# Seven products of halves for a part of the first DFT, the second DFT as a stage of its own, and block sums made by transfers

## The chip, the cores and the metric

The kernel runs on one core of one Trainium2 chip, all in 32-bit floating point. The metric is device time in microseconds (us) of one execution. The kernel before takes 946.69 us, the median of three runs (946.5 to 949.13).

## What is computed

One block of a network on x of 2048 rows s by 512 columns d (the batch is 1):

```
def _A_ref(x, dft_seq_re, dft_seq_im, dft_hid_re, dft_hid_im):
    a = jnp.einsum("bsd,ed->bse", x, dft_hid_re)
    b = jnp.einsum("bsd,ed->bse", x, dft_hid_im)
    return jnp.einsum("ts,bse->bte", dft_seq_re, a) - jnp.einsum("ts,bse->bte", dft_seq_im, b)

def _B_ref(x, w_in, w_sp, b_sp, w_out):
    z = _gelu(jnp.einsum("bsd,df->bsf", x, w_in))             # f: 2 * 896
    z1, z2 = z[..., :896], _layernorm(z[..., 896:], axis=-1)
    g = jnp.einsum("ts,bsf->btf", w_sp, z2) + b_sp[None, :, None]   # w_sp: 2048 x 2048
    return jnp.einsum("bsf,fd->bsd", z1 * g, w_out)

mod = (_silu(c) @ w_mod).reshape(c.shape[0], 6, 1, -1)
sa, ca, ga, sb, cb, gb = (mod[:, j] for j in range(6))
h = _layernorm(x, axis=-1) * (1 + ca) + sa
x = x + ga * _A_ref(h, A_dft_seq_re, A_dft_seq_im, A_dft_hid_re, A_dft_hid_im)
h = _layernorm(x, axis=-1) * (1 + cb) + sb
x = x + gb * _B_ref(h, B_w_in, B_w_sp, B_b_sp, B_w_out)
```

The kernel turns the order of the two transforms round: it first forms G = (C h), with C the real and the imaginary matrix over the rows s, and then multiplies G by the small matrices over the columns d.

## The kernel before

**Products.** A float32 factor is split into a high part (a copy in the TensorE's format, made by ScalarE) and a low part (the rest, made by VectorE), and each product of tiles is three matmuls, high by high, high by low and low by high (`matmul3`, lines 95 to 97). A matmul has 128 x 128 weights and 512 columns.

**Stages.** (1) The first DFT, tiles `gp`. The 2048 output positions are four row blocks t of 512. For each t and each of the real and imaginary matrices (j) there are 16 steps over s, 128 steps n in all, and a step is 4 column blocks of 128 by 3 matmuls, 12 matmuls. Its matrix arrives in blocks of 512 x 512 (tile `stage`, 1 MB, four transfers), which VectorE turns 32 x 32 by 32 x 32 (tile `t`) before ScalarE makes the high half (`ah`, line 256) and VectorE the low one (`al`, line 263). (2) The second DFT, tiles `yp`, 384 matmuls on G, which stays on the chip as `gh` and `gl`; its pieces are called between the steps of stage 1, a row block later. (3) z1 and z2, the two halves of the product with w_in. (4) The product with w_sp, tiles `gw`, as seven products of halves: it needs sums of quarters of w_sp, which VectorE makes from tiles `sj` and stores to `s_d` (`load_s`, `sum_s`, lines 756 to 769). (5) The product with w_out, tiles `op`.

**After a piece of the second DFT** (`post_y`, `norm_y`, `post_h`) VectorE adds the residual (`xr`) and takes mean and variance (`bn_stats`, lines 103 to 105), GpSimd makes the reciprocal root from them in three tiny instructions (`mvy`, `rsy`, `nmry`: lines 107, 108, 115), ScalarE normalizes (line 119), two elementwise passes multiply and add the modulation rows (lines 579, 580), and the result goes to DRAM.

**Order.** The engines run their instructions in the order in which the program writes them. A table (`at(n, function, arguments)`) says after which step n a piece of side work is written; `run(n)` writes it, and `prep(n)` writes the preparation of the factors some steps ahead. Tiles rotate through a fixed number of buffers (`bufs=`), and an instruction that writes a tile waits until the readers of the buffer's last tile are done. The SP queue issues the loads of the stages, the GpSimd (POOL) queue the stores and a few loads.

## Time and profile before

| | |
|---|---|
| median of three runs | 946.69 us |
| the profiled execution, first to last instruction | 945.0 us |
| TensorE busy | 938.0 us, 99% |
| VectorE busy | 707.0 us, 75% |
| ScalarE busy | 386.9 us, 41% |
| GpSimd busy | 177.4 us, 19% |
| moved by transfers | 161.79 MB, 171 GB/s over the span |
| first real matmul starts at | 8.01 us |
| last matmul starts at | 941.27 us |

The span is the time between the first and the last instruction of one execution that the profiler recorded; its 945.0 us lie 1.7 us below the median of the unprofiled runs. "Busy" is a sum over instructions whose ends can overlap the next one's start, so what one instruction costs in a row of instructions is read from start to start. The DMA share of a stretch is the mean busy share of the core's 16 transfer engines, and can come out a little over 1. In the table of groups, "idle before" is the time in which an engine stood still ahead of the group's instructions, with what ended the wait behind the arrow.

### The profile page before, as it was taken

The numbers are of one execution on the slowest core, as the hardware profiler recorded it, in microseconds if no ns is written. First come the engines' busy times: TensorE is split into PE (matmuls) and PEld (weight loads), VectorE is DVE, ScalarE is ACT, GpSimd is POOL, SyncE is SP. The second block draws the span as 40 slices with busy tenths as digits, with TensorE's granted clock in tenths as the row PEclk, the third lists the DMA queues.
The fourth block names the chain that finished last, engine by engine and source line by source line (L and its number), as shares of the span: only waits on it lengthen the run. The fifth ranks groups of instructions, "written<-read, shape, count | busy, mean of one in ns | idle before, by whom it ended". The sixth has DMA issues, their size and how long they took to land.

```text
span 945.0 us, 12296 instructions
## 1 busy us (share of the span) xinstructions
PE 938.0 (99%) x4158; PEld 780.9 (83%) x4158; DVE 707.0 (75%) x1048; ACT 386.9 (41%) x670; POOL 177.4 (19%) x333
## 2 busy tenths in 40 slices
PE   8999999999999999999999999999999999999998
PEld 6878888888888888888888999888888888888886
DVE  7789957775765657767978587877688688885872
ACT  3685424232232222322876356544544444331221
POOL 1430000221631145122323265200000000000000
PEclk9999999999999999999999999999999999999999
DMA  8998653577668965996398985555554456833541
GB/s 194 222 214 165 130 134 90 146 197 158 134 101 197 281 208 150 279 281 141 95 344 282 326 267 160 149 114 134 124 134 90 106 117 141 205 107 117 198 155 59
DMA packets 253230, 161.79 MB, mean 171 GB/s; under 512 B 134576, under 2 KB 222896, under 8 KB 253040
## 3 DMA queue, kind: packets, MB, share of 16 engines
q1 hardware_dynamic: 238544, 120.62, 53.7%
q0 software_dynamic: 12272, 39.61, 12.3%
q10 hardware_dynamic: 2352, 0.79, 0.3%
q8 instruction: 32, 0.52, 0.3%
q14 instruction: 30, 0.25, 0.1%
HBM read 124.26 MB, written 36.71 MB: 170 GB/s over the span
## 4 chain that ended last, share of the span: by engine, by line
PE 94%; DMA 2%; SPq 1%; issue 1%; POOL 1%; DVE 0%; ACT 0%; ACTq 0%; DVEq 0%; POOLq 0%
PE gp L96 11%; PE gp L97 11%; PE gp L95 11%; PE gw L95 10%; PE gw L96 10%; PE gw L97 10%; PE yp L97 3%; PE yp L96 3%; PE yp L95 3%; PE z2p L96 3%; PE z2p L95 3%; PE z2p L97 3%; PE op L97 3%; PE op L95 3%; PE op L96 3%; PE z1p L96 1%
## 5 line engine op out<-in xcount | busy, mean ns | idle before, releaser
L256 ACT ACTIVATE ah<-t 128x512 fp32r<-128x512 f32 x263 | 164.4, 627 | 310.2 <-PE gp L97 181.0
L263 DVE TENSOR_TENSOR al<-t,ah 128x512 fp32r<-128x512 f32 x264 | 179.9, 685 | 133.4 <-PE gp L96 59.8
L96 PE MATMUL gp<-al,hh 128*128 128x512 f32 x480 | 186.8, 389 | 1.2 <-DVE al L263 1.2
L97 PE MATMUL gp<-ah,hl 128*128 128x512 f32 x480 | 186.8, 389 | 0.0
L95 PE MATMUL gp<-ah,hh 128*128 128x512 f32 x480 | 186.7, 389 | 0.0
L97 PE MATMUL gw<-ah,bl 128*128 128x512 f32 x400 | 155.6, 389 | 0.0
L96 PE MATMUL gw<-al,bh 128*128 128x512 f32 x400 | 155.6, 389 | 0.0
L95 PE MATMUL gw<-ah,bh 128*128 128x512 f32 x400 | 155.6, 389 | 0.0
L96 PEld LDWEIGHTS gp<-al,hh 128*128 128x128 f32 x480 | 90.1, 188 | 20.4 <-DVE al L263 1.6
L95 PEld LDWEIGHTS gp<-ah,hh 128*128 128x128 f32 x480 | 90.1, 188 | 18.7
L97 PEld LDWEIGHTS gp<-ah,hl 128*128 128x128 f32 x480 | 90.1, 188 | 18.8 <-DVE hl L448 0.2
L97 PEld LDWEIGHTS gw<-ah,bl 128*128 128x128 f32 x400 | 75.1, 188 | 15.7
L95 PEld LDWEIGHTS gw<-ah,bh 128*128 128x128 f32 x400 | 75.1, 188 | 15.5
L96 PEld LDWEIGHTS gw<-al,bh 128*128 128x128 f32 x400 | 75.1, 188 | 15.5
L227 DVE STREAM_TRANSPOSE t<-stage 128x1024 f32<-128x1024 f32 x62 | 76.7, 1238 | 8.7 <-DMA stage<-in_A_dft_seq_re_dram 8.6
L221 DVE STREAM_TRANSPOSE t<-stage 128x1024 f32<-128x1024 f32 x56 | 69.3, 1238 | 0.1
L791 ACT ACTIVATE bh<-z 128x512 fp32r<-128x512 f32 (+1 forms) x56 | 32.8, 586 | 65.7 <-PE gw L96 65.7
L769 POOL DMA_DIRECT2D s_d<-sj x64 | 35.1, 550 | 107.5 <-DVE sj L761 80.7
L95 PE MATMUL yp<-hth,gh 128*128 128x512 f32 x128 | 49.8, 389 | 0.0
L96 PE MATMUL yp<-htl,gh 128*128 128x512 f32 x128 | 49.8, 389 | 0.0
L97 PE MATMUL yp<-hth,gl 128*128 128x512 f32 x128 | 49.8, 389 | 0.0
L96 PE MATMUL z2p<-wil,ah 128*128 128x448 f32 x128 | 46.7, 365 | 0.0
(210 smaller groups left out, 1448.0 us busy)
## 6 DMA issues: line engine op xcount, KB each, us to landing
sj<-in_B_w_sp_dram SPq DMA_DIRECT2D x32, 512.0 KB, 8.3
s_d<-sj POOLq DMA_DIRECT2D x64, 256.0 KB, 4.1
stage<-s_d SPq DMA_DIRECT2D x128, 128.0 KB, 2.9
stage<-in_A_dft_seq_re_dram SPq DMA_DIRECT2D x60, 256.0 KB, 5.4
stage<-in_A_dft_seq_im_dram SPq DMA_DIRECT2D x60, 256.0 KB, 5.9
stage<-in_B_w_sp_dram SPq DMA_DIRECT2D x96, 128.0 KB, 3.1
stage<-h_d SPq DMA_DIRECT2D x32, 256.0 KB, 6.4
xr<-in_A_x_dram POOLq DMA_DIRECT2D x16, 256.0 KB, 4.3
```

The source lines that it names most:

```text
L95: nc.tensor.matmul(acc, ah, bh, start=first, stop=False, skip_group_check=go_on)
L96: nc.tensor.matmul(acc, ah, bl, start=False, stop=False, skip_group_check=go_on)
L97: nc.tensor.matmul(acc, al, bh, start=False, stop=last, skip_group_check=go_on)
L221: nc.vector.transpose(t.rearrange("p r (b i) -> p r b i", i=32), st[:, :, :, 16 * k:16 * k + 32])
L227: nc.vector.transpose(t.rearrange("p k (b i) -> p k b i", i=32), st[:, :, 32 * k:32 * k + 64].rearrange("p b (k i) -> p k b i", k=2))
L256: nc.scalar.activation(AH[n], source(n), AF.Copy)
L263: nc.vector.tensor_tensor(AL[n], source(n), AH[n].bitcast(F32), op=ALU.subtract)
L769: nc.gpsimd.dma_start(s_d[m, r, g][b * P:(b + 1) * P, :], a)
L791: nc.scalar.activation(BH[p, k][:, :w], b_of(p, k), AF.Copy)
```

## The change

The first DFT's row block t = 0 stays as it was. For t = 1, 2, 3 the rows s of the lower half (8 of the 16 tiles), the four column blocks (as 2 x 2) and the two matrices' rows are taken as quarters, and a 2 x 2 by 2 x 2 product of quarters is made from seven products of sums of them (`mm_s`, 14 units of 12 matmuls) where eight were needed; the upper half is multiplied directly onto the same accumulators (`mm_k`, 8 units of 24 matmuls). A row block is then 168 + 192 = 360 matmuls and was 384. VectorE makes the sums of the matrix blocks (`sum_f`, 128 x 1024) and of h (`sum_v`). Factors are split as pairs of two steps, 128 x 1024 at once (`hi_unit`, `lo_unit`).

G no longer stays on the chip: it goes to DRAM (`out_g`, `out_k`, tiles `go` with two buffers, stores on the POOL queue) and is read back in 16 pieces (`load_g`). The second DFT is a loop of 16 pieces m after the first (`mm_y`, 24 matmuls each); the residual is copied into its accumulator ahead (`seed_y`), and the gate `mods[2]` is multiplied into the small matrix (`gate_ht`), so that the statistics are taken from the accumulator directly.

The sums of quarters of w_sp are no longer made by VectorE: rows are loaded, negated by ScalarE, stored, and summed in DRAM by 32 accumulating transfers of 512 KB, beside 24 plain stores and 8 copies from DRAM to DRAM of that size, all on the POOL queue and written at steps 29 to 98. Two of the seven products take the opposite sign in their splits (`hi_b`, `lo_b`).

The core of the diff:

```
-        if s == NS - 1:
-            for k in range(ND):
-                ps = GP.pop((t, j, k))
-                gt_hi[t, j, k] = GP_[0].tile([P, Q], F32R, tag=f"gh{j}_{k}", name=f"gh{t}_{j}_{k}")
-                gt_lo[t, j, k] = GP_[0].tile([P, Q], F32R, tag=f"gl{j}_{k}", name=f"gl{t}_{j}_{k}")
-                split(gt_hi[t, j, k], gt_lo[t, j, k], ps)
...
+    def pair_of(d, u, name):
+        if u not in d:
+            d[u] = pairs.tile([P, 2, Q], F32R, tag=name, bufs=3, name=f"{name}{u}")
+        return d[u]
...
+    def sum_f(t, p, m):
...
+        dst, a, b, op = {5: (f5, b12, b22, ALU.add), 7: (b12, b11, b12, ALU.subtract),
+                         6: (b11, f5, b11, ALU.subtract), 3: (b21, b21, b11, ALU.subtract)}[p]
+        nc.vector.tensor_tensor(dst, a, b, op=op)
...
+    def out_g(t, c, ps):
+        g = temp(f"go{t}_{c}")
+        nc.scalar.activation(g, ps, AF.Copy)
+        nc.gpsimd.dma_start(g_d[t][c], g)
...
+    def mm_s(t, i):
+        p, m = ORD[i // 2], i % 2
+        acc = {1: "c11", 2: "c11", 5: "v", 3: "v", 6: "u", 7: "u", 4: "u"}[p]
...
+        for c_ in range(2):
+            for f in range(2):
+                matmul3(C[acc, f], *form_v(p, 2 * m + c_, f), ph[:, c_, :], pl[:, c_, :],
+                        p in (1, 5) and m == 0 and c_ == 0, m == 1 and c_ == 1, p not in (1, 5))
...
+    def mm_k(t, i, m):
...
+        for k in range(ND):
+            acc = (("c11", "v"), ("u", "c22"))[j][k // 2]
+            matmul3(C[acc, k % 2], h_hi[s][:, k, :], h_lo[s][:, k, :], ph, pl, False, s == 7, True)
+
+    def out_k(t, j):
+        for f in range(2):
+            out_g(t, 4 * j + f, C["u" if j else "c11", f])
+        for f in range(2):
+            um = UM[t][:, 2 * j + f, :]
+            nc.vector.tensor_tensor(um, C["c22" if j else "v", f], um, op=ALU.add)
+            nc.gpsimd.dma_start(g_d[t][4 * j + 2 + f], um)
...
+    def load_g(m):
+        t, i = divmod(m, 4)
+        GR[m] = yp[0].tile([P, 8, P], F32, tag="gr", bufs=2, name=f"gr{m}")
+        nc.sync.dma_start(GR[m], g_d[t].rearrange("c p s -> p c s")[:, :, i * P:(i + 1) * P])
...
+    def split_g(m):
+        GH[m] = yp[0].tile([P, 8, P], F32R, tag="gh", bufs=3, name=f"gh{m}")
+        GL[m] = yp[0].tile([P, 8, P], F32R, tag="gl", bufs=2, name=f"gl{m}")
+        split(GH[m], GL[m], GR.pop(m))
...
+    def negate_s(b):
+        n = SJ.pop(b)
+        for j in range(2):
+            nc.scalar.activation(n[:, j], n[:, j], AF.Copy, scale=-1.0)
+        nc.gpsimd.dma_start(s_rows(1, b), n[:, 0])
+        nc.gpsimd.dma_start(s_rows(3, b), n[:, 0])
+        nc.gpsimd.dma_start(s_rows(2, b), n[:, 1])
+
+    def add_s(dst, src_):
+        nc.gpsimd.dma_start(dst, src_, accum_op=ALU.add)
...
+    for role, l, n, m in ((21, 5, 9, 11), (11, 7, 13, 15), (12, 12, 17, 19), (22, 16, 21, 23)):
+        atd(l, load_first, role)
+        atd(n, turn_s, 1, role, 0)
+        atd(m, turn_s, 1, role, 1)
...
+    for b, n in enumerate((29, 32, 35, 58, 61, 64, 67, 70)):
+        atd(n, load_s, b)
+        atd(n + 3, negate_s, b)
+        atd(n + 1, copy_s4, b)
+        atd(n + 8, sum_s1, b)
+        atd(n + 9, sum_s3, b)
+        atd(n + 18, sum_s2, b)
+        atd(n + 28, sum_s4, b)
...
+    for m in range(16):
+        n = Y0 + 2 * m
+        atd(n - 3, split_g, m)
+        atd(n - 2, seed_y, m)
+        if m + 2 < 16:
+            atd(n - 2.5, load_g, m + 2)
+            atd(n - 1.5, load_xr, m + 2)
+        atd(n + 2, post_y, m)
+        atd(n + 3, norm_y, m)
+        atd(n + 4, post_h, m)
```

**The order on VectorE around a piece of the second DFT.** Before, from line 568 (the product's gate) over the statistics to the low halves and turns of the first DFT that are woven in:

```order
L566 TENSOR_TENSOR y_0_1786<-yp_0_1_1757,y_0_0_1425 128x512
L568 TENSOR_TENSOR y_0_1786<-y_0_1786,mod_1732 128x512
L569 TENSOR_TENSOR xr_0_1666<-y_0_1786,xr_0_1666 128x512
L103 BN_STATS bsty<-xr_0_1666 128x6
L105 BN_AGGR mvy<-bsty 128x2
L263 TENSOR_TENSOR al_1800<-t_1736,ah_1772 128x512
L227 STREAM_TRANSPOSE t_1802<-stage_1645 128x1024
```

In the changed kernel, in the loop over m (`gl` is the low half of a piece of G, `h_2` and `h_3` the pieces normalized by ScalarE, `wl` and `wraw` the preparation of w_in):

```order
L105 BN_STATS bsty<-yp_3184 128x6
L107 BN_AGGR mvy<-bsty 128x2
L918 TENSOR_TENSOR wl_3258<-wraw_0_3125,wh_3257 128x1024
L93 TENSOR_TENSOR gl_3309<-gr_3206,gh_3308 128x1024
L826 TENSOR_TENSOR h_3_3306<-h_3_3306,mod_2755 128x512
L827 TENSOR_TENSOR h_3_3306<-h_3_3306,mod_2757 128x512
L105 BN_STATS bsty<-yp_3235 128x6
L107 BN_AGGR mvy<-bsty 128x2
L918 TENSOR_TENSOR wl_3313<-wraw_2_3130,wh_3312 128x1024
L93 TENSOR_TENSOR gl_3364<-gr_3260,gh_3363 128x1024
L904 TENSOR_TENSOR wraw_0_3125<-wraw_0_3125 128x2x384
L826 TENSOR_TENSOR h_4_3361<-h_4_3361,mod_2755 128x512
```

And on ScalarE in that loop, where `x_3` is the copy of the accumulator that goes to DRAM and line 806 the copy of the residual:

```order
L817 ACTIVATE x_3_3277<-yp_3184 128x512
L806 ACTIVATE yp_3289<-xr_3186 128x512
L121 ACTIVATE h_3_3306<-x_3_3277,nmry,rsy 128x512
L92 ACTIVATE gh_3308<-gr_3206 128x1024
L915 ACTIVATE wh_3312<-wraw_2_3130 128x1024
L817 ACTIVATE x_4_3332<-yp_3235 128x512
```

What stood behind the statistics was work of the first DFT; what stands there now is `gl`, the low half of the piece of G that TensorE takes two pieces later, and it reads `gh`, which ScalarE writes behind the normalization of the same statistics.

**The order on VectorE at the start.** Before, around the statistics of x's third quarter (`bstx<-x_399`):

```order
L263 TENSOR_TENSOR al_529<-t_486,ah_511 128x512
L227 STREAM_TRANSPOSE t_531<-stage_338 128x1024
L103 BN_STATS bstx<-x_399 128x6
L105 BN_AGGR mvx<-bstx 128x2
...
L263 TENSOR_TENSOR al_570<-t_486,ah_538 128x512
L263 TENSOR_TENSOR al_593<-t_531,ah_572 128x512
L227 STREAM_TRANSPOSE t_595<-stage_448 128x1024
```

In the changed kernel (`pl` is the low half of a pair, `f_21` a quarter for the seven products of t = 1, whose block `sb_426` is loaded at step 5):

```order
L543 STREAM_TRANSPOSE tp_509<-stage_312 128x1024
L471 TENSOR_TENSOR hl_528<-xn_416,hh_498 128x512
L543 STREAM_TRANSPOSE f_21_531<-sb_426 128x1024
L105 BN_STATS bstx<-x_399 128x6
L107 BN_AGGR mvx<-bstx 128x2
...
L619 TENSOR_TENSOR pl_565<-tp_509,ph_563 128x1024
L543 STREAM_TRANSPOSE tp_567<-stage_340 128x1024
```

A turn of a block of the next row block now stands ahead of the statistics and of the pair that steps 14 and 15 multiply.

**The order of the POOL queue at steps 40 to 60.** Before, it held the first loads of the residual and, some steps on, the stores of x:

```order
L504 DMA w_1_1419<-hrow_d_132 128x512
L544 DMA xr_0_1666<-in_A_x_dram 128x512
L544 DMA xr_1_1711<-in_A_x_dram 128x512
L570 DMA x_d_76<-xr_0_1666 128x512
L107 TENSOR_SCALAR mvy<-mvy 128x1
```

Now, with `s_d` the sums of w_sp, `go` the copies of G and `um` the kept products that G's other half is made from:

```order
L1015 DMA s_d_0_95<-s_d_0_97 128x1024
L1015 DMA s_d_0_99<-in_B_w_sp_dram 128x1024
L1015 DMA s_d_0_97<-s_d_0_99 128x1024 x2
L654 DMA g_d_77<-go_0_1550 128x512
L654 DMA g_d_77<-go_1_1553 128x512
L708 DMA g_d_77<-um_1154 128x512 x2
L1015 DMA s_d_0_97<-s_d_0_99 128x1024
L1015 DMA s_d_0_101<-s_d_0_97 128x1024
```

The stores of G of the row block t = 1 stand behind the transfers that sum w_sp.

718 lines of the change are left out of this document (451 added, 267 removed).

## The prediction, made before the changed kernel was run

> **What bounds the kernel now.** I read the page first (the span, the engines' sums, the DMA queues, the chain that ended last, the costliest groups):
>
> ```profile
> span 945.0 us, 12296 instructions
> ...
> PE 938.0 (99%) x4158; PEld 780.9 (83%) x4158; DVE 707.0 (75%) x1048; ACT 386.9 (41%) x670; POOL 177.4 (19%) x333
> ...
> q1 hardware_dynamic: 238544, 120.62, 53.7%
> q0 software_dynamic: 12272, 39.61, 12.3%
> ...
> PE 94%; DMA 2%; SPq 1%; issue 1%; POOL 1%; DVE 0%; ACT 0%; ACTq 0%; DVEq 0%; POOLq 0%
> ...
> L96 PE MATMUL gp<-al,hh 128*128 128x512 f32 x480 | 186.8, 389 | 1.2 <-DVE al L263 1.2
> ```
>
> TensorE is the bound: 99% busy, 94% of the chain, and its largest group waited 1.2 us in all. Then the table by stretch (PE busy and its count, PEld, DVE, ACT, POOL, granted clock, DMA share, GB/s):
>
> ```profile
> 40.00:50.00 10.00, 9.40 (x42) 7.46 (x40) 3.58 (x8) 4.69 (x11) 4.14 (x14) 1.00 1.19 226
> 50.00:60.00 10.00, 9.38 (x41) 7.79 (x42) 9.82 (x15) 9.50 (x22) 2.74 (x9) 1.00 1.21 210
> ...
> 150.00:200.00 50.00, 50.00 (x222) 41.39 (x221) 38.84 (x58) 16.83 (x28) 6.98 (x14) 1.00 0.55 138
> ```
>
> A full TensorE does 222 matmuls in 50 us, 0.225 us each at clock 1.00 (the 389 ns are overlapping ends). The two stretches at 40 to 60 us show the one place where it waits, 0.6 us each; transfers are saturated there (share 1.2). So a removed matmul is worth 0.225 us, and only where the other engines keep up with the shorter work.
>
> **The gain.** Stage 1 loses 24 matmuls in each of three row blocks, 72 of 4158: 72 x 0.225 = 16.2 us. Nothing else leaves TensorE. In stages 3 to 5 what changes is the signs of two splits and 45 us of VectorE's sums, off the path while TensorE is full: nothing. Against the profiled execution that is 945.0 - 16.2 = 928.8 us if TensorE stays full.
>
> **The second DFT as a loop.** This is where I think it doesn't. Before, the statistics of a piece had a whole row block of other work behind them. Now a piece m costs TensorE 24 x 0.225 = 5.40 us, and the engines beside it form a ring: statistics of piece m on VectorE, three GpSimd instructions, normalization on ScalarE, and behind that in ScalarE's order the high half of G's piece m + 3; VectorE's next instruction is the low half of this piece, then the two modulation passes of piece m, and only then the statistics of m + 1. The links, from one piece before, engine by engine (start, length):
>
> ```profile
> 176.67 0.69 DVE L103 BATCH_NORM_STATS2 bsty<-xr 128x6 f32<-128x512 f32 x1
> 177.40 0.18 DVE L105 BATCH_NORM_AGGREGATE mvy<-bsty 128x2 f32<-128x6 f32 x1
> ```
>
> ```profile
> 177.68 0.54 POOL L107 TENSOR_SCALAR mvy<-mvy 128x1 f32<-128x1 f32 x1 [0.20 <-DVE mvy L105]
> 178.31 0.56 POOL L108 TENSOR_TENSOR rsy<-mvy,mhalf 128x1 f32<-128x1 f32 x1
> 178.97 0.27 POOL L115 TENSOR_SCALAR nmry<-mvy,rsy 128x1 f32<-128x1 f32 x1
> ```
>
> ```profile
> 179.27 0.82 ACT L119 ACTIVATE h<-xr,nmry,rsy 128x512 f32<-128x512 f32 x1 [1.37 <-POOL nmry L115]
> 179.99 0.62 ACT L256 ACTIVATE ah<-t 128x512 fp32r<-128x512 f32 x1
> ```
>
> Statistics to normalization is 179.27 - 176.67 = 2.60 us here. GpSimd's part varies (min/median/max in ns over all 16 pieces):
>
> ```profile
> L107 POOL TENSOR_SCALAR mvy<-mvy x16: 182/524/793, 177.7 to 452.8; 128x1 f32<-128x1 f32 x16
> L108 POOL TENSOR_TENSOR rsy<-mvy,mhalf x16: 559/895/1285, 178.3 to 453.7; 128x1 f32<-128x1 f32 x16
> L115 POOL TENSOR_SCALAR nmry<-mvy,rsy x16: 265/266/1796, 179.0 to 455.1; 128x1 f32<-128x1 f32 x16
> ```
>
> With the shortest mvy it is 2.60 - 0.36 = 2.24 us, with the three medians 2.60 - 0.02 + 0.34 = 2.92. Normalization holds ScalarE for 179.99 - 179.27 = 0.72 us. The halves of G's piece are 128 x 1024, whose rows are (the first on ScalarE, the second on VectorE):
>
> ```profile
> L668 ACT ACTIVATE wh<-wraw x3: 1043/1062/1062, 435.5 to 459.6; 128x1024 fp32r<-128x1024 f32 x3
> ```
>
> ```profile
> L671 DVE TENSOR_TENSOR wl<-wraw,wh x3: 1217/1219/1225, 436.6 to 462.3; 128x1024 fp32r<-128x1024 f32 x3
> ```
>
> that is 1.06 and 1.2 us, with 0.1 for the hop between (an estimate from the 0.20 above, which holds half of the statistics' own tail). The modulation passes take 449.77 - 448.47 = 1.30:
>
> ```profile
> 448.47 0.66 DVE L579 TENSOR_TENSOR h<-h,mod 128x512 f32<-128x512 f32 x1
> 449.16 0.69 DVE L580 TENSOR_TENSOR h<-h,mod 128x512 f32<-128x512 f32 x1
> 449.77 0.69 DVE L263 TENSOR_TENSOR al<-t,ah 128x512 fp32r<-128x512 f32 x1
> ```
>
> The ring is 2.24 + 0.72 + 1.06 + 0.1 + 1.2 + 1.3 = 6.6 us at least, 7.3 with the medians, 7.0 in the middle, against TensorE's 5.4: 1.6 us late per piece. The first piece in the ring, m = 3, starts with a lead: its low half is done 6.9 us after TensorE ends piece 0 (1.2 us for m = 2's half, which had waited for that buffer, then 4.5 us of ring and 1.2), and is needed 10.8 us after it, so 3.9 us of slack (4.2 with the short ring, 3.6 with the long). Twelve pieces follow: 12 x 1.6 - 3.9 = 15.3 us of stalls (10.4 and 19.4 at the ends). Five preparations of w_in and of z1 stand in the ring as well, between a low half and the modulation: two sums and one low half of 128 x 768, a sum in two parts, a low half of 128 x 512:
>
> ```profile
> 458.29 0.42 DVE L655 TENSOR_TENSOR wraw<-wraw,wraw 128x256 f32<-128x256 f32 x1
> 458.62 0.95 DVE L657 TENSOR_TENSOR wraw<-wraw,wt 128x768 f32<-128x768 f32 x1
> ```
>
> 3 x 0.95 + 0.42 + 0.95 + 0.69 = 4.9 us. **Together 20 us (15 to 24).** What is late next is nothing: z1 prepares its first factors in the same loop.
>
> The Trainium skill bears on GpSimd's part ("GPSIMD Engine Reference", Specifications): its path to the chip's memory is shared with VectorE, and they contend while VectorE reads two inputs from there. The spread of mvy, 182 to 793 ns, fits that. By it GpSimd would run at its shortest here, since VectorE mostly stands still while it waits in the ring: 15 us in place of 20, and a time 5 us lower than mine.
>
> **The start.** VectorE's list now has the turn of a block of t = 1 ahead of the statistics of x's third quarter and of the pair for steps 14 and 15. That block is the tenth megabyte in the SP queue's order. The tenth before was the block that VectorE waited 6.35 us for:
>
> ```profile
> 48.75 1.25 DVE L227 STREAM_TRANSPOSE t<-stage 128x1024 f32<-128x1024 f32 x1 [6.35 <-DMA stage<-in_A_dft_seq_re_dram]
> ```
>
> ```profile
> 50.62 0.50 PE L96 MATMUL gp<-al,hh 128*128 128x512 f32 x1 [1.22 <-DVE al L263]
> ```
>
> At the same rate it lands at about 47 to 48.75 us; the turn (1.25), the statistics of two tiles (2 x 0.9) and the pair's low half (1.2) end at 51 to 53 us, while step 14 would start at 8.0 + 14 x 12 x 0.225 = 45.8 by the first real matmul:
>
> ```profile
> 8.01 1.17 PE L468 MATMUL gp<-ah,hh 128*128 128x512 f32 x4 [0.86 <-DVE ah L959]
> ```
>
> Two further halves stand behind it. I take 7 us of stalls for the 1.2 of now, **6 us more** (0 if the block comes early enough, 10 at most).
>
> **The sums of w_sp by transfers.** They ran on VectorE's results between 299 and 589 us:
>
> ```profile
> L769 POOL DMA_DIRECT2D s_d<-sj x64: 539/539/627, 299.2 to 588.7; - x64
> ```
>
> and move to steps 29 to 98, roughly 76 to 265 us. That stretch and its POOL transfers before (MB, share):
>
> ```profile
> 76.00:265.00 189.00, 189.00 (x836) 156.49 (x835) 141.73 (x203) 66.34 (x118) 36.62 (x58) 1.00 0.62 140
> ```
>
> ```profile
> q0 software_dynamic: 2080, 6.30, 12.7%
> ```
>
> The transfer engines are free for 0.38 x 189 = 72 us. Added are 8.4 MB of rows, 24 stores, 8 copies and 32 accumulations of 0.52 MB, 42 MB, and 5 MB of G; the POOL queue's price over the program is 0.123 x 945 / 39.61 = 2.9 us per MB, so 137 us; 0.127 x 189 = 24 us leave. Demand passes the free time by 41 us, by 90 if an accumulation costs double (its target is read as well; no row shows one). The sums themselves have time until stage 4. What it costs is in the queue behind them: the stores of G, whose two buffers `go` are written next by VectorE (`wt`) and ScalarE in their order. I see two such places, steps 53 and 84, each nothing if the queue is less than about 5 us late there and up to 12 us if it isn't; **8 us for both** (0 to 24).
>
> Sum: 945.0 - 16.2 + 20 + 6 + 8 = 962.8 us; the median of the runs is 1.7 above the profile, so **964.5 us**.
>
> **The rivals.** (1) TensorE stays full: the ring is no longer than 5.4 us or the lead lasts. 945.0 - 16.2 + 0 to 6, with the 1.7: 930.5 to 937. For it: VectorE and ScalarE have room by their sums (75%, 41%). Against it: the ring's six links at their shortest add up to 6.6. Chance 0.12. (2) Cheap on all sides, the short ring and little elsewhere: 945.0 - 16.2 + 15.3 + 0 to 6 + 1.7 = 946 to 952, at best 941 if half of the five preparations find a gap. Chance 0.14; a third of it within the bound, a quarter below. (3) The transfers decide: once the POOL queue is over 5 us late at step 53, VectorE stands in its order before a buffer, the pairs run out, and it comes again at 84 and in the loads that SP holds behind the same tiles; 20 us each in place of 4: 964.5 + 32, 985 to 1000. For it is the overflow of 41 to 90 us, against it that the start lived with a share of 1.2. Chance 0.13. The Trainium skill speaks for this one ("DMA: Bandwidth & Descriptors", Queues, rings and completion order): an engine goes round between queues packet by packet. By the two queue rows of the profile's page a packet of q1 takes 0.537 x 945 x 16 / 238544 = 34 ns of an engine and one of q0 152, so with both backlogged the stage loads would be left with some 18% of the engines.
>
> **How the numbers follow.** The forecast, 952 to 982, has 0.61. The range for 8 in 10 takes in rival 2 and half of rival 3: 941 to 988. What this kernel's measurement can tell from no change is 0.3%, 2.8 us. Faster by more: 0.12 + 0.04 = 0.16; within: 0.05 and 0.03 from the forecast's low edge, 0.08; slower: 0.76.
>
> **What would show it.** In the loop (TensorE's last 384 matmuls of the two DFTs) a wait of TensorE for `gl` of 1 to 2 us in nearly every piece from the sixth on, and starts of the statistics 7 us apart, show the ring; starts 5.4 apart with no wait break it, and then I am wrong by 20 us. A wait of VectorE for `sb` before 49 us and of TensorE for `pl` behind it show the start. Waits for `go` buffers by ScalarE or VectorE at 150 to 240 us, and the share at 1.1 or more through that stretch, show the transfers; TensorE full there makes them free. 72 matmuls fewer in TensorE's count, at 0.225 each in any stretch where it is full, show the gain.

## The result and the profile after

The changed kernel takes 1069.29 us, the median of four runs (1068.91 to 1070.43); the kernel before, in the same comparison, 946.84. The ratio is 1.129, with a 95% interval of 1.128 to 1.131: 13% slower, where the prediction had 964.5 and a range up to 988.

The page of the profiled execution after (the span, the engines' sums, the granted clock in 40 slices, and the POOL queue):

```profile
span 1067.4 us, 12027 instructions
...
PE 952.4 (89%) x4086; PEld 778.0 (73%) x4086; DVE 708.3 (66%) x957; ACT 450.4 (42%) x710; POOL 177.6 (17%) x355
...
PEclk9999968989769989999899999999999999999999
...
q0 software_dynamic: 19024, 64.78, 22.0%
```

TensorE has its 72 matmuls fewer (4086 for 4158) and yet 952.4 us of busy time for 938.0; it is busy for 89% of the span and was for 99%. No other engine comes near to full. The POOL queue's (q0's) share has gone from 12.3% to 22.0%, and the clock, which was 1.00 throughout, falls to 0.6 in two slices of the span and to 0.7 in a third.

Where the time went is read from the first matmul of each stage. The rows of the tile views give them, after and then before (duration in ns, first and last start):

```profile
L97 PE MATMUL gs_c<-ph,hh x144: 388/389/792, 103.2 to 451.5; 128*128 128x512 f32 x144
L97 PE MATMUL yp<-hth,gh x128: 387/389/796, 452.2 to 562.2; 128*128 128x512 f32 x128
L97 PE MATMUL z1p<-ah,wh x32: 389/389/628, 562.9 to 613.7; 128*128 128x512 f32 x32
L97 PE MATMUL z2p<-wih,ah x128: 362/365/369, 637.5 to 714.7; 128*128 128x448 f32 x128
```

```profile
L95 PE MATMUL z1p<-ah,wh x32: 389/389/389, 447.2 to 491.7; 128*128 128x512 f32 x32
L95 PE MATMUL z2p<-wih,ah x128: 362/365/369, 515.5 to 592.7; 128*128 128x448 f32 x128
```

| stretch, us | before | after | difference | the prediction's terms |
|---|---|---|---|---|
| first DFT, t = 0, from 8.0 | 87.6 | 95.2 | +7.6 | +6 |
| first DFT, t = 1 to 3 | 265.2 | 349.0 | +83.8 | -16.2 + 8 |
| second DFT | 86.4 | 110.7 | +24.3 | +20 |
| z1 | 68.3 | 74.6 | +6.3 | 0 |
| z2 to the end | 429.5 | 429.9 | +0.4 | 0 |
| sum | 937.0 | 1059.4 | +122.4 | +17.8 |

(Before, the two DFTs were interleaved. Its 87.6 is 384 matmuls at 0.225 us and the 1.2 us wait, its 86.4 is 384 at 0.225, and 265.2 is what is left of the time to 447.2. The start is taken at 8.0 us in every run.) Four of the five rows came out within 7 us of their terms. The fifth is the miss. From 265.2 less the 16.2 of the removed matmuls to 349.0 there are **100 us too many in t = 1 to 3**, where the prediction had 8.

The table by stretch, for t = 1 to 3 and for the second DFT (PE busy and count, PEld, DVE, ACT, POOL, granted clock, DMA share, GB/s):

```profile
103.00:452.00 349.00, 264.65 (x1092) 210.72 (x1090) 206.84 (x221) 125.35 (x170) 68.77 (x108) 0.89 0.92 224
452.00:563.00 111.00, 95.65 (x387) 74.80 (x386) 65.10 (x93) 47.18 (x67) 41.80 (x86) 0.95 0.71 216
```

In the first row TensorE stands for 349.0 - 264.65 = 84 us, and its 1092 matmuls take 264.65 where 1092 x 0.225 is 245.7: another 19 us. The same two differences in the second row are 15 us and 95.65 - 387 x 0.225 = 8.6 us. How much of the 19 and of the 8.6 is the lower clock is worked out further down.

The waits of TensorE say what it stood for (total, times, longest); under them are two waits of ScalarE and the POOL queue for each other, which the prediction had argued about:

```profile
PE gs_u L98 <- DVE pl L619: 35.2, 6, 22.3
PE gs_c L97 <- ACT ph L615: 22.5, 3, 20.9
PE gs_v L97 <- ACT ph L615: 21.1, 2, 17.5
PE yp L97 <- ACT yp L806: 15.3, 10, 2.7
PE z1p L97 <- ACT z1g L939: 4.5, 1, 4.5
...
ACT go L653 <- DMA g_d<-go: 11.1, 4, 6.0
POOL g_d L654 <- ACT go L653: 134.5, 14, 46.9
```

70 of the 84 us in t = 1 to 3 are four long stops for factors. In the timeline (start, length, idle before and its releaser) each of them goes back to a load on the SP queue that landed late. The first three:

```profile
159.43 1.25 DVE L543 STREAM_TRANSPOSE f<-stage 128x1024 f32<-128x1024 f32 x1 [23.44 <-DMA stage<-in_A_dft_seq_im_dram]
161.84 0.79 PE L98 MATMUL gs_u<-pl,hh 128*128 128x512 f32 x1 [22.30 <-DVE pl L619]
...
273.30 2.00 ACT L1009 ACTIVATE sj<-sj 128x1024 f32<-128x1024 f32 x2 [20.83 <-DMA sj<-in_B_w_sp_dram]
276.30 0.80 PE L97 MATMUL gs_v<-ph,hh 128*128 128x512 f32 x1 [17.51 <-ACT ph L615]
...
317.81 1.25 DVE L543 STREAM_TRANSPOSE tp<-stage 128x1024 f32<-128x1024 f32 x1 [25.84 <-DMA stage<-in_A_dft_seq_re_dram]
320.28 0.79 PE L97 MATMUL gs_c<-ph,hh 128*128 128x512 f32 x1 [20.91 <-ACT ph L615]
```

At 273 us it is ScalarE that stands, in its order, before the negation of a row of w_sp that has not landed (`negate_s`), and the next `ph` behind it is late. The fourth long stop, 9.1 us up to 378 us, goes back to a block of w_mod (`wb`) that VectorE waited 10.7 us for. Around the first stop the SP queue reads (a row's length is that of its issues):

```profile
122.90 10.28 SPq L162 DMA_DIRECT2D stage<-in_A_dft_seq_im_dram  x4
133.41 23.89 SPq L162 DMA_DIRECT2D wb<-in_w_mod_dram  x4
157.40 4.83 SPq L162 DMA_DIRECT2D stage<-in_A_dft_seq_re_dram  x4
```

and the two queues in the 24 us from the second row on (packets, MB, share of the engines), with the landing of the last of the four loads of the first row:

```profile
q0 software_dynamic: 1345, 4.90, 86.6%
q1 hardware_dynamic: 2311, 1.15, 19.6%
...
stage<-in_A_dft_seq_im_dram SPq DMA_DIRECT2D x1, 256.0 KB, 34.7
```

The POOL queue, with the transfers of the sums, holds 86.6 of 106.2 parts of the engines, and the SP queue with the loads that TensorE lives on gets 19.6, which is 18%. A load of 256 KB, which in the median of the program lands in 7 us, took 34.7, and the four issues of the next tile (a block of w_mod) took 23.9 us, six on average: nothing behind them on SP could start. That is the share worked out under the prediction's third rival, from the two packet lengths and the round of packets that the Trainium skill describes ("DMA: Bandwidth & Descriptors", Queues, rings and completion order); this trace agrees with it.

The SP queue also stood by itself, 40.5 us in all at two places, for a buffer `sj` that a store on the POOL queue had to leave first. Those waits ended at 115.9 and 237.6 us, and after both the next load of the matrix still had a buffer of its own to wait for, until 122.9 and 244.5; so they did not set its time.

### The profile page after: what moved, and what is told of

Its sections match the earlier page's. It is cut to its first block, busy times and chain, and to the rows that moved or that the text cites. A ratio compares the mean times of both kernels' runs of the same rounds, so it can differ in the third digit from the quotient of the medians.

```text
span 1067.4 us, 12027 instructions
## 1 busy us (share of the span) xinstructions
PE 952.4 (89%) x4086; PEld 778.0 (73%) x4086; DVE 708.3 (66%) x957; ACT 450.4 (42%) x710; POOL 177.6 (17%) x355
## 4 chain that ended last, share of the span: by engine, by line
PE 48%; DVE 6%; DMA 3%; issue 3%; ACT 2%; POOL 1%; SPq 0%; DVEq 0%; ACTq 0%; POOLq 0%
PE gw L99 9%; PE gw L98 8%; PE gw L97 8%; PE z2p L97 2%; PE z2p L98 2%; PE z2p L99 2%; PE op L99 2%; PE op L98 2%; PE op L97 2%; DVE gl L93 1%; PE z1p L97 1%; DMA stage<-in_A_dft_seq_im_dram 1%; PE z1p L99 1%; ACT gh L92 1%; PE z1p L98 1%
## 5 line engine op out<-in xcount | busy, mean ns | idle before, releaser
L270 DVE TENSOR_TENSOR al<-t,ah 128x512 fp32r<-128x512 f32 x136 | 92.8, 688 | 96.4 <-PE gw L98 45.4
L263 ACT ACTIVATE ah<-t 128x512 fp32r<-128x512 f32 x136 | 84.9, 626 | 98.7 <-PE gw L99 56.8
L619 DVE TENSOR_TENSOR pl<-f,ph 128x1024 fp32r<-128x1024 f32 x42 | 50.8, 1212 | 49.3 <-ACT ph L615 49.2
L97 PE MATMUL gs_c<-ph,hh 128*128 128x512 f32 x144 | 56.9, 395 | 22.5 <-ACT ph L615 22.5
L543 DVE STREAM_TRANSPOSE tp<-stage 128x1024 f32<-128x1024 f32 x36 | 44.6, 1239 | 40.7 <-DMA stage<-in_A_dft_seq_re_dram 33.0
L228 DVE STREAM_TRANSPOSE t<-stage 128x1024 f32<-128x1024 f32 x56 | 69.4, 1239 | 1.2 <-DMA stage<-in_B_w_sp_dram 1.1
L98 PE MATMUL gs_c<-pl,hh 128*128 128x512 f32 x144 | 57.0, 396 | 2.4 <-DVE pl L619 2.4
L619 DVE TENSOR_TENSOR pl<-tp,ph 128x1024 fp32r<-128x1024 f32 x35 | 42.7, 1221 | 22.0 <-ACT ph L615 22.0
L99 PE MATMUL gs_c<-ph,hl 128*128 128x512 f32 x144 | 56.5, 392 | 0.0
L615 ACT ACTIVATE ph<-f 128x1024 fp32r<-128x1024 f32 x42 | 43.6, 1052 | 13.8 <-DVE f L584 4.4
## 6 DMA issues: line engine op xcount, KB each, us to landing
sj<-in_B_w_sp_dram SPq DMA_DIRECT2D x8, 1024.0 KB, 10.4
```

The source lines that it names most:

```text
L97: nc.tensor.matmul(acc, ah, bh, start=first, stop=False, skip_group_check=go_on)
L98: nc.tensor.matmul(acc, ah, bl, start=False, stop=False, skip_group_check=go_on)
L99: nc.tensor.matmul(acc, al, bh, start=False, stop=last, skip_group_check=go_on)
L228: nc.vector.transpose(t.rearrange("p r (b i) -> p r b i", i=32), st[:, :, :, 16 * k:16 * k + 32])
L263: nc.scalar.activation(AH[n], source(n), AF.Copy)
L270: nc.vector.tensor_tensor(AL[n], source(n), AH[n].bitcast(F32), op=ALU.subtract)
```

## The experiments

Thirteen kernels were run; e1 to e9 (there is no e4) are one run each, e10 to e14 medians of four to ten. The table has the device time, and the same five stretches of each profiled execution as above; what differs from the row after by more than a few us is in bold. In e1, e11, e12 and e14 the sums of w_sp are left out, and in e2 they are copies, so that these five are measures and not versions of the kernel.

| run | device time | t = 0 | t = 1 to 3 | second DFT | z1 | z2 to the end |
|---|---|---|---|---|---|---|
| before | 946.84 | 87.6 | 265.2 | 86.4 | 68.3 | 429.5 |
| after | 1069.29 | 95.2 | 349.0 | 110.7 | 74.6 | 429.9 |
| e1, no sums | 972.40 | 95.6 | **251.6** | 110.3 | 75.2 | 429.9 |
| e2, plain copies for sums | 1028.29 | 95.5 | **309.4** | 112.3 | 71.4 | 429.9 |
| e5, G stored from ScalarE's queue | 1073.66 | 95.5 | 353.1 | 111.1 | 74.5 | 429.7 |
| e3, halves of G a half step earlier | 1059.86 | 95.0 | 349.9 | **100.9** | 74.4 | 429.9 |
| e6, halves, seed and loads earlier | 1078.04 | 97.2 | 348.3 | 109.2 | **83.6** | 429.9 |
| e7, sums spread to stage 4 | 1028.44 | 94.8 | **282.8** | 113.0 | 74.5 | **453.6** |
| e8, start of t = 1 later | 1067.33 | **89.6** | 353.0 | 110.4 | 74.6 | 429.9 |
| e9, e6 to e8 together | 1035.99 | **89.2** | **289.5** | 110.4 | **83.8** | **453.3** |
| e10, ring in three pieces, sums wider | 1001.35 | **90.3** | **287.1** | **104.5** | 79.7 | 430.4 |
| e11, as e10, no sums | 950.97 | **89.9** | **251.0** | **89.9** | 80.0 | 429.9 |
| e12, as e11, z1 prepared earlier | 951.82 | **89.8** | **251.1** | **90.7** | 79.1 | 429.9 |
| e13, as e12, sums on VectorE, later | 989.11 | **90.0** | **251.4** | **90.4** | **91.3** | **455.8** |
| e14, as e12, z1's copies first | 945.69 | **90.3** | **250.5** | **90.2** | 75.3 | 429.9 |

### What the sums cost: e1, e2, e5

e1 leaves the sums out; stage 4 then loads quarters of w_sp of the same size in their place:

```diff
-    for b, n in enumerate((29, 32, 35, 58, 61, 64, 67, 70)):
-        atd(n, load_s, b)
...
-        atd(n + 28, sum_s4, b)
```

> Left out: the sums of quarters of w_sp, with all their loads, stores, copies and accumulating transfers; stage 4 loads quarters of w_sp in their place, as many bytes. Theory A (the w_sp transfers hold the transfer engines, loads on the SP queue starve, TensorE stops and its clock is halved after each stop): the row blocks t = 1 to 3, 349 us in the changed kernel against 243 for their 1080 matmuls at 0.225, fall to 243 to 260, and the whole to 960 to 980. Theory B (the new work of VectorE and ScalarE in the first DFT is too long in their order, whatever the transfers do): over 300 us for the three row blocks, the whole over 1020.

The time falls by 97 us, all of it in t = 1 to 3, whose 251.6 us stand against 249.0 for before's stretch less the gain. The table by stretch of e1 for it (columns as above):

```profile
103.00:355.00 252.00, 248.99 (x1094) 204.63 (x1093) 205.82 (x220) 109.39 (x152) 22.87 (x42) 1.00 0.65 149
```

TensorE stands for 3 us in all, at clock 1.00, and the share of the transfer engines is 0.65 where it was 0.92. So 97 of the 100 us are the sums', and the new products of halves themselves run at TensorE's rate.

e2 keeps every transfer with its bytes and lets it copy in place of adding:

```diff
-        nc.gpsimd.dma_start(dst, src_, accum_op=ALU.add)
+        nc.gpsimd.dma_start(dst, src_)
```

> The 32 accumulating transfers become plain ones between the same places: the same bytes, order and waits, and wrong sums. If an accumulation costs twice a plain transfer because it reads its target too, the stops shrink by a third to a half: 1015 to 1040. If it is the number of bytes and the time at which they are asked for, nothing much changes: 1050 to 1072.

So 41 us are the adding, and 56 over e1 stay with plain transfers. The page's rows of q0 in e1 (span 970.6) and in e2 (span 1026.5) give the price of each:

```profile
q0 software_dynamic: 9808, 31.22, 9.0%
```

```profile
q0 software_dynamic: 19024, 64.78, 18.4%
```

The 64 transfers of 0.52 MB hold the 16 engines for 0.220 x 1067.4 - 0.090 x 970.6 = 147 us in the kernel after and for 0.184 x 1026.5 - 0.090 x 970.6 = 102 us as plain ones. If all plain ones cost the same, that is 1.6 us for a plain one, 3.0 us per MB, and 3.0 us for one that adds: nearly double.

e5 takes the stores of G out of the POOL queue, behind which the prediction saw the danger:

```diff
         nc.scalar.activation(g, ps, AF.Copy)
-        nc.gpsimd.dma_start(g_d[t][c], g)
+        nc.scalar.dma_start(g_d[t][c], g)
```

> The stores of the copies of G (tiles go) are issued by ScalarE's queue and no longer by the POOL queue, behind whose w_sp transfers they stood; all else is the same. By the prediction's step (buffers of go that wait for stores stuck in the POOL queue) the row blocks t = 1 to 3 fall from 349 to under 290 us, the whole under 1015. By theory A (loads that starve) they stay at 335 to 352 us, the whole at 1055 to 1072.

Nothing is gained (353.1 for 349.0, a little over the range of theory A), although ScalarE's waits for `go` fall from 11.1 us to 2.6. The buffers `go` were not what held the engines in the long stops. The rows of the waits above say the same: the POOL queue's stores of G waited 134.5 us for ScalarE's copies, up to 46.9, and ScalarE 11.1 us for the stores, none of it ahead of a long stop. The queue held ScalarE once more, 5.5 us up to 224.8, for a small store of a modulation row (`row_d`), but behind it in ScalarE's order stood a negation whose row of w_sp landed only at 225.7.

### The ring in the second DFT: e3, e6, and its part of e10 and e11

In the kernel after, a turn of the ring from 502.49 to 510.54 (VectorE, ScalarE and the matmul that waits; other rows are left out):

```profile
502.49 0.69 DVE L105 BATCH_NORM_STATS2 bsty<-yp 128x6 f32<-128x512 f32 x1
...
505.40 0.82 ACT L121 ACTIVATE h<-x,nmry,rsy 128x512 f32<-128x512 f32 x1 [1.10 <-POOL nmry L117]
...
506.13 1.04 ACT L92 ACTIVATE gh<-gr 128x1024 fp32r<-128x1024 f32 x1
507.20 1.23 DVE L93 TENSOR_TENSOR gl<-gr,gh 128x1024 fp32r<-128x1024 f32 x1 [2.89 <-ACT gh L92]
508.34 0.95 DVE L904 TENSOR_TENSOR wraw<-wraw,wraw 128x768 f32<-128x768 f32 x1
...
509.93 0.69 DVE L827 TENSOR_TENSOR h<-h,mod 128x512 f32<-128x512 f32 x1
510.54 0.69 DVE L105 BATCH_NORM_STATS2 bsty<-yp 128x6 f32<-128x512 f32 x1
...
511.26 0.60 ACT L817 ACTIVATE x<-yp 128x512 f32<-128x512 f32 x1 [4.10 <-DVE bsty L105]
511.76 0.60 ACT L806 ACTIVATE yp<-xr 128x512 f32<-128x512 f32 x1
512.41 0.80 PE L97 MATMUL yp<-hth,gh 128*128 128x512 f32 x1 [2.29 <-ACT yp L806]
```

The links are those of the prediction, in its order: statistics to normalization 2.91 us, 0.73 of ScalarE, the high half, the low half, a preparation of w_in, the two passes. It is 8.05 us with the preparation and 7.1 without. But the link that lets TensorE go is another: ScalarE copies x out of the accumulator behind the statistics of the same accumulator (4.10 us of wait), and the seed of a later piece (`seed_y`, `yp<-xr`) stands behind that copy. TensorE waits for the seed, and not for `gl`.

e3 writes the halves of G a half step earlier, ahead of the normalization:

```diff
-        atd(n - 3, split_g, m)
+        atd(n - 4, split_g, m)
```

> The halves of G's piece m are written one half step earlier, so that ScalarE makes the high half ahead of the normalization and not behind it. If the ring of statistics, GpSimd, normalization, high half, low half and modulation sets the pace of the second DFT (110.7 us for 86.4 us of matmuls), this stage falls to 86 to 92 us and the whole by 18 to 26 us, to 1043 to 1052. If it is something else there (loads of G, the copy of the residual by itself, the slower clock), the stage stays above 105 us.

The second DFT falls from 110.7 to 100.9, between the two forecasts: 9.8 of the 24.3 us that the ring cost. What stays is the copy, the seed and both halves between the statistics and the modulation passes: in the trace of e3 the statistics start at 480.19 and next at 486.62, 6.4 us apart with a 1.1 us preparation. e6 moves everything of a piece ahead:

```diff
-        atd(n - 3, split_g, m)
-        atd(n - 2, seed_y, m)
+        atd(n - 4.5, split_g, m)
+        atd(n - 5, seed_y, m)
         if m + 2 < 16:
-            atd(n - 2.5, load_g, m + 2)
-            atd(n - 1.5, load_xr, m + 2)
+            atd(n - 4, load_g, m + 2)
+            atd(n - 4.5, load_xr, m + 2)
```

> In the second DFT both halves of G's piece are written ahead of the statistics of the piece before, and the copy of the residual into the accumulator two and a half steps ahead of the piece that needs it, so that nothing TensorE waits for stands behind statistics. If the ring and the five preparations in it are all that slows this stage, it goes from 110.7 us (100.9 with the halves moved alone) to 86 to 90, and the whole to 1043 to 1050. If VectorE's or ScalarE's own work is the limit there, it stays over 97.

This missed: 109.2. Each high half stands behind a normalization in ScalarE's order here as well, and z1 became 9 us longer. It took a split of the pair: the high half at n - 4.5, the low one at n - 4, the seed at n - 5. In e11 the ring so written is broken; two starts of the statistics in a row, after which the third comes at 413.08:

```profile
401.31 0.69 DVE L105 BATCH_NORM_STATS2 bsty<-yp 128x6 f32<-128x512 f32 x1
...
407.02 0.69 DVE L105 BATCH_NORM_STATS2 bsty<-yp 128x6 f32<-128x512 f32 x1
```

5.7 to 6.1 us apart with preparations in it, TensorE's waits in the whole stage are 1.7 us, and the second DFT takes 89.9 us where TensorE alone needs 86.4. Against the 110.3 of e1, which has no sums either, the ring's price was 20.4 us.

### The places of the transfers and the start: e7, e8, e9, e10

e7 writes each of the first three groups of sums in steps of 3, from step 92 on, and the fourth group in stage 4 (the loads of the rows and two small loads also move by up to four steps):

```diff
-        atd(n + 1, copy_s4, b)
-        atd(n + 8, sum_s1, b)
-        atd(n + 9, sum_s3, b)
-        atd(n + 18, sum_s2, b)
-        atd(n + 28, sum_s4, b)
+    for b in range(8):
+        atd(92 + 3 * b, sum_s1, b)
+        atd(93.5 + 3 * b, sum_s3, b)
+        atd(Y0 + 5 + 3 * b, sum_s2, b)
+        at(N4 + 2 + 2 * b, copy_s4, b)
+        at(N4 + 3 + 2 * b, sum_s4, b)
```

> The same sums of w_sp, but only the loads of its rows, the negations and the 24 stores stay in the row blocks t = 1 and 2 (and these a little further apart); the 32 accumulations and 8 copies are written from step 92 on, through t = 3, the second DFT and the first two products of stage 4. Theory A (transfer engines held, loads starve): t = 1 to 3 falls from 349 to 255 to 285 us, since 21 of 42 MB and all accumulations leave the crowded part, and the whole to 980 to 1010. If the stops come from the loads and the negations in ScalarE's order instead (a ScalarE that waits for a load of rows), the stops at 260 to 320 us stay: over 315 us, the whole over 1035.

t = 1 to 3 lose 66 us of their 100, as theory A had it; the whole, 1028.44, misses its range, because stage 4 gets a stop that was nowhere before:

```profile
712.46 0.81 POOL L1015 DMA_DIRECT2D s_d<-s_d  x1 [5.87 <-DMA s_d<-in_B_w_sp_dram]
713.00 0.87 POOL L1123 DMA_DIRECT2D wor<-in_B_w_out_dram  x1
...
718.41 0.69 DVE L1126 TENSOR_TENSOR wor<-wor,mod 128x512 f32<-128x512 f32 x1 [23.25 <-DMA wor<-in_B_w_out_dram]
...
719.76 0.80 PE L98 MATMUL gw<-al,bh 128*128 128x512 f32 x1 [19.44 <-DVE al L270]
```

VectorE stands in its order before a block of w_out, but this load is not one that starved. It is issued by the POOL queue, at 713.00 us, and VectorE goes on 5.4 us after that. It was late because it stood behind the sums on that queue: each adding transfer waits there until the copy that it adds to has landed (5.87 us for the one shown, 5.2 to 10.5 for the five before it). That is the danger that the prediction saw, work behind the sums on their own queue, with another victim. So e7 shows two things: with the adding transfers out of t = 1 and 2, and half of them and the copies out of t = 3 too, most of the starving there is gone, and a queue that waits for its own transfers stops whatever stands behind them.

e8 moves the first turns of t = 1 behind the statistics and pairs of t = 0:

```diff
-    for role, l, n, m in ((21, 5, 9, 11), (11, 7, 13, 15), (12, 12, 17, 19), (22, 16, 21, 23)):
+    for role, l, n, m in ((21, 8, 14, 15), (11, 10, 16, 17), (12, 15, 19, 21), (22, 17, 23, 25)):
```

> The four blocks for the first seven products are loaded some steps later (first at step 8, not 5) and turned at steps 14 to 25, not 9 to 23. If the prediction's step on the start is right (VectorE stands before a block that has not landed, with the pair of step 14 behind it), the first row block, 95.2 us now from 8.0 to 103.2, falls to 87 to 90, the whole by 5 to 8 us. If the transfers of the start are simply too many, it stays at 94 to 96.

t = 0 falls by 5.6 us, as the term of 6 asked, but the whole by 2 only: t = 1 to 3, with the sums still in them, take 4 us longer. e9 joins e6, e7 and e8:

> The last three edits together, all of the result computed. By the sum of their parts: 1069 - 22 (second DFT) - 6 (start) - 70 to 95 (transfers) = 946 to 971. Under 944 it would be faster than the kernel before.

It missed, at 1035.99: the gains of e7 and e8 add up, but e7's stop in stage 4 and the miss of e6 are in it. e10 has the ring of three pieces, the start of e8, and the sums 6 to 8 steps apart (`sum_s1` at 92 + 6b, `sum_s3` at 95 + 6b, `sum_s2` at 142 + 8b, the fourth group from N4 + 1 on in steps of 8):

> All of the result computed. The start as in the run before on it; the accumulations and copies spread further: 16 over steps 92 to 137, 8 over 142 to 198, and the 8 copies with their 8 accumulations over 64 steps of stage 4, four steps between any two there; the negations one or two steps later. In the second DFT the high half of piece m + 4 now stands behind the normalization of m, and the low half of m + 3 behind its statistics, so that no chain from statistics to the next statistics is longer than 4.5 us beside TensorE's 5.4. If the ring was the cause this stage falls to 86 to 92 us. If crowding (how many w_sp transfers per time) starves the loads, the wait of 20 us in stage 4 goes and t = 1 to 3 come to 250 to 275; the whole 938 to 965. If accumulations stop the loads however far apart they are, stage 4 keeps 15 us or more of waits and the whole stays over 985.

1001.35 us, a ratio of 1.058 (1.056 to 1.059): over both ranges of the theory of crowding, and over the 985 of the other one, whose waits in stage 4 are not there. So neither fits whole. Stage 4 no longer stops, but t = 1 to 3 stand at 287.1, 36 us above e11, with the eight rows, their 24 stores and the first ten adding transfers still in it. The second DFT, 104.5 us, is 15 us above e11 as well: TensorE waits 10.4 us there for high halves of G, whose loads are late.

### What is left with the sums away: e11, e12, e14, and the sums elsewhere: e13

e11 is e10's order without the sums:

> The same, with the sums of w_sp left out altogether (stage 4 loads quarters of w_sp instead). What the change is worth without its transfers: 945.0 - 16.2 for the matmuls, 1 to 3 for the start, 0 to 5 each for the three row blocks, the second DFT and the beginning of z1: 930 to 945 by the profile, 932 to 947 by the median, faster than before. Over 955 there is a cause that I have not seen yet.

950.97, a ratio of 1.0045 (1.0028 to 1.0062), 4 us over the top of its range. With the whole cost of the sums away and ring and start mended, the kernel is still not faster than before; the largest piece of what is lost is z1, whose one wait, for `z1g`, has grown from 4.5 to 9.9 us.

e12 prepares z1's factors some steps earlier (a load, the turns, a sum and the halves of the first step, two to four steps ahead of where they were):

> As the last run without the sums of w_sp, and with the preparations of z1 that stood on VectorE between the statistics of the last pieces (a turn and three sums) some steps earlier. In that run z1 took 79.9 us against 68.3 in the kernel before, with a wait of 9.9 us for a copy of accumulators that waited for the last piece's statistics. If that is the rest of the loss, z1 falls to 68 to 72 and the whole from 948.7 to 937 to 942 by the profile, ratio to before 0.988 to 0.997: the change is then worth about 0.5 to 1% once the four places are mended, and its sums free. If z1 is slow for another reason, it stays at 946 to 950.

A miss: 79.1 for 80.0. The wait is not for factors, it is for `z1g`, a copy that ScalarE makes of the first accumulators; ScalarE comes to it behind the normalization of the last piece. e14 makes that normalization one step later, and with it the modulation of pieces 13 to 15, so that the last statistics come earlier:

```diff
-        atd(n + 3, norm_y, m)
-        atd(n + 4, post_h, m)
+        atd(n + (4 if m == 15 else 3), norm_y, m)
+        atd(n + (5 if m > 12 else 4), post_h, m)
```

> As the last run without the sums of w_sp, with the end of the second DFT reordered: statistics of pieces 14 and 15 ahead of the modulation of 13 and 14, and z1's copies of its accumulators ahead of the normalization of piece 15. If the wait of 9 us at the start of z1 is the queue behind the last statistics, z1 falls from 79 us to 68 to 73 and the whole from 948.6 to 937 to 943 by the profile, ratio 0.989 to 0.998. If it is something else, 946 to 950.

z1 falls to 75.3, still above its range, and the wait to 4.4 us. The ratio is 0.9984 (0.9974 to 0.9994), a gain of 0.16%, which is under the 0.3% that the prediction took as the least that can be told from no change. This is the change at its best, without a part of the work: t = 1 to 3 are 14.7 us shorter than before, and t = 0 (+2.7), the second DFT (+3.8) and z1 (+7.0) give 13.5 of them back.

e13 asks whether the sums can be had elsewhere: VectorE makes them from tiles, as before the change, in z1, z2 and early in stage 4, with 16.8 MB of loads and 64 stores and no adding transfers:

```diff
+    for i in range(16):
+        u = i // 4 % 2, i // 8, i % 4
+        c = (13, 16)[i] if i < 2 else 28 + 1.6 * (i - 2)
+        at(N2 + int(c), load_sj, *u)
+        at(N2 + int(c) + 2, sum_sj, *u, True)
+        at(N2 + int(c) + 3, sum_sj, *u, False)
```

> All of the result computed: the same, with the sums of w_sp made by VectorE as in the kernel before, but in z1, z2 and the first steps of stage 4, where there is room on the chip (16.8 MB of loads and as much in 64 stores within about 130 us, no accumulation). If only accumulations and DRAM-to-DRAM copies starve the loads, the three DFT stages are as in the run without sums and z1, z2 and stage 4 lose little: 938 to 950. If the bytes per time decide whatever their kind, z2 and stage 4 lose 10 to 30 us: 950 to 970.

989.11, a ratio of 1.046 (1.044 to 1.048), dearer than expected: from z1 on it takes 38 us more than e12 (12 in z1, 26 behind it).

```profile
PE gw L98 <- DVE al L270: 15.0, 5, 8.4
...
PE z1g L98 <- DVE al L270: 8.0, 1, 8.0
```

These two waits of TensorE, for factors, were not there in e12. VectorE, which makes the factors, stands in its order before tiles `sj` of w_sp that have not landed, 31.8 us in five waits:

```profile
DVE sj L1030 <- DMA sj<-in_B_w_sp_dram: 31.8, 5, 10.3
```

A tile is loaded only two steps ahead of its sums here. Whether the transfers are too dense or the loads too late, no run tells apart. Before the change the same sums cost nothing, spread over 290 us (299 to 589) in which TensorE was busy throughout and the transfer engines had a share of 0.77. No version that computes everything and has the new DFT beat the kernel before; the best is e13. How far a placing of the sums through the whole program could go is open: it wasn't tried.

## Why the prediction was wrong, step by step

**The gain** was right: 72 matmuls fewer, and 14.7 of the 16.2 us appear in e14, where TensorE is full.

**The start** was right in its main place: VectorE waits 7.2 us for `sb`, TensorE 2.9 us for `pl` behind it, and e8 takes 5.6 us back. That the size came out, 7.6 for 6, is in part luck. TensorE's other waits there, 2.7 us in three, are for low halves of h (`hl`), which no term had, and a stretch at clock 0.50 from 51.4 to 54.8 us makes the rest longer:

```profile
47.90 1.25 DVE L543 STREAM_TRANSPOSE f<-sb 128x1024 f32<-128x1024 f32 x1 [7.22 <-DMA sb<-in_A_dft_seq_re_dram]
...
PE gp L98 <- DVE pl L619: 2.9, 1, 2.9
```

**The ring** was there, and its size nearly right: 20 predicted in a range of 15 to 24, 24.3 measured. Part of that is luck, since two errors lay in it. The last link is the seed behind the copy of x and not `gl`, and what was worked out as stalls alone was in fact 15 us of stalls and 8.6 us in which the matmuls took longer. The Trainium skill's sentence on the memory path that GpSimd shares with VectorE ("GPSIMD Engine Reference", Specifications) agrees with this trace at two places: `mvy` took 0.18 us where VectorE stood and 0.79 where it worked on two inputs (at 511.61 and 503.57). The time 5 us lower that I worked out by it did not come: the total was longer, not shorter.

**"What is late next is nothing"** was wrong by 6.3 us. z1's factors were ready (e12 took only 0.9 us off z1); what is late is ScalarE, whose copies of z1's first accumulators stand behind the last piece's normalization. TensorE waits 4.5 us for them. With the ring mended the wait was 9.9 and z1 80.0 us; e14, which changes that order, has 4.4 and 75.3. No run took the wait away altogether. The 2 us besides are, by the count of matmuls from 563 to 638 us (304 in 70.5 us, where 68.4 are due), slower matmuls after it.

**The sums of w_sp, "8 us for both"**, is the step that failed: 100 us, 97 of them by e1. The working up to that step was sound. It found the transfer engines short by 41 us, and by 90 if an adding transfer costs double, and 2.9 us per MB for the queue; the runs give 3.0 us per MB, and nearly double for adding. The demand of the 64 transfers, 147 us, passes the 252 x 0.35 = 88 us which the transfers of e1 leave free in t = 1 to 3 by 59 us, and the rows' 8.4 MB on the SP queue come on top of it. The error came after that: the overflow was allowed to wait until stage 4, as if only the POOL queue's own work could be late, and a price was set on the two places behind that queue. But the engines serve both queues, and what was late was the other queue, SP's, with the loads that TensorE lives on. e5 shows that the place that I priced is not where the time went; the 18% and the 34.7 us at 133 to 157 us show the one that I didn't price. How the 100 us divide between late landings and held issues on the SP queue, no run tells.

**The third rival** named it, "and in the loads that SP holds behind the same tiles", with the share of 18% beside it, and I gave it 0.13 and a price of 20 us at two places. Of its mechanism only this last part ran; its beginning, VectorE before a buffer that waits for the POOL queue, is not what the long stops go back to. Its price was short for two reasons: there were four stops of 9 to 22 us and some small ones, 84 us, and the matmuls took another 19 us longer, most of it after the longer stops at half the clock.

**The clock** is in no term of the prediction; it was 1.00 all through before. After five of the stops it is 0.50 for some microseconds. The first of these stretches and the sum of all five (161.8 to 167.4, 228.9 to 235.7, 276.3 to 280.0, 320.3 to 324.4 and 378.0 to 382.4 us, the clock 0.50 in each):

```profile
161.80:167.40 5.60, 5.56 (x13) 4.40 (x14) 2.25 (x2) 0.00 (x0) 0.00 (x0) 0.50 1.11 227
...
sum 24.60, PE 23.05 PEld 17.30 DVE 20.05 ACT 13.12 POOL 6.86; mean PE 4.61 PEld 3.46 DVE 4.01 ACT 2.62 POOL 1.37
```

13 matmuls take 5.56 us in the first, 0.43 each. The Trainium skill says this ("TensorE: Matmul & The Clock Gate", HAM oscillation: idle gaps over some 3.4 us bring half the clock back), and a term for it was there to be had. The five stops ahead, 3.6 to 22.3 us, are all longer than that. TensorE works for 23.05 us in these stretches, and at the full clock it would take half of that: by this estimate 11.5 of the 19 us are the clock's, on 84 of stops. Part of the rest is that the last matmul before a wait counts with its whole 0.39 us; I did not split it further. The ring shows that shorter gaps are followed by it too (last section); there the same working gives 4.9 of the 8.6 us.

With the five prices set right the sum is 945.0 - 16.2 + 100.0 + 24.3 + 7.6 + 6.3 + 0.4 = 1067.4. It must close, since the prices are the differences of the stretches; that the causes behind them are right rests on the runs above.

## What to carry to other kernels

Where work is moved to the transfer engines, add up their time in the stretch into which it goes, adding transfers at double, and where that passes what is free there, charge the whole overflow to whoever waits for loads, whatever queue these are on: a backlog on one queue leaves the other its share of packets only, here 18%. Then look at what stands behind them on their own queue, as the load of w_out did in e7. An order of loads and sums that hides well behind a full engine is worth more than the matmuls that a shorter algorithm saves; here the removed 72 matmuls are 1.7% of the time, and even in e14 the three seams that came with them (the start, the ring of small steps, the hand-over to z1) take nearly all of it back. A stop of TensorE costs its length and often some of the clock: here about 12 us on 84.

## What was not expected of the hardware

- **The issue itself is held.** With the engines backlogged, four issues of 256 KB on the SP queue took 23.9 us and four others 25.3 (at 133 and 291 us), where four take 4.8 us at the end of the first stop: the queue is blocked, not only its data.
- **An adding transfer from DRAM to DRAM** of 0.52 MB holds the 16 engines for 3.0 us, a plain one for 1.6 (e2 against the kernel after).
- **Gaps of 1.8 to 2.7 us can bring the lower clock.** In the second DFT TensorE stands from 494.45 to 497.18 us; its matmuls start about 0.225 us apart until 498.45, then 0.43 apart until 501.80, and then 0.225 again. Gaps of 2.3 us (up to 512.41) and 1.8 us (up to 527.77) have such a stretch behind them too:

```profile
498.50:501.90 3.40, 3.40 (x10) 2.62 (x9) 1.85 (x3) 2.22 (x3) 0.80 (x2) 0.50 0.39 154
512.40:515.50 3.10, 3.09 (x7) 2.48 (x8) 0.87 (x1) 1.76 (x2) 1.42 (x4) 0.50 1.19 241
529.30:532.60 3.30, 3.30 (x9) 2.62 (x8) 2.23 (x2) 1.04 (x2) 0.00 (x0) 0.50 0.49 159
```

The first drop comes 1.3 us after the work has begun again and lasts 3.4 us. Gaps of 1.7 us (up to 488.70) and 2.0 us (up to 557.29) brought none, and in e1 neither did one of 2.7 us (up to 399.8). So the 3.4 us that the Trainium skill gives is no lower bound here, and the length of one gap alone does not decide; what does, no run tells.
